# Dealing the first loads of a fused attention and GLU kernel to three DMA queues, and storing its last tile in three pieces

## The chip, the core and the metric

The kernel runs on one core of one Trainium2 chip. The metric is the device time of one execution in microseconds; the profile's span is about 1.8 us shorter, since it starts with the first instruction. The median of the kernel before is 222.75 us. A run counts as slow here when it is more than 1.5% above the fastest run of the same kernel; ratios use the others, the fast runs alone, and the text says where a run is slow. The engines are called TensorE (PE in the profile; its weight loads are PEld), VectorE (DVE), ScalarE (ACT), GpSimd (POOL) and SyncE (SP).

## The reference

2048 tokens of 512 features are normalized, go through a linear attention with a softmax feature map (32 heads of 16 features) and, beside it, through a bilinear GLU of 1792 columns; the sum of both and the input is the output.

```python
xn = layernorm(x)                      # x: (1, 2048, 512), bf16
q, k, v = split(xn @ wqkv)             # wqkv: (512, 1536)
pq, pk = q @ w_phi, k @ w_phi          # per head, 16 x 16
phi_q = concat(softmax(pq), softmax(-pq)); phi_k = likewise
o = (phi_q @ (phi_k.T @ v)) / (phi_q @ sum(phi_k) + 1e-6)
out = x + o @ wo + ((xn @ w_gate) * (xn @ w_up)) @ w_down
```

## The kernel before

The kernel folds w_phi into the k part of wqkv ("W1k", from wk transposed and a block-diagonal BD made of wphi), so the first things that it needs are four token tiles (statistics on VectorE, transpose on TensorE), wv, then wk transposed and wphi, then the first 256 columns of the two GLU weights, wg and wu. A DMA is started by SyncE, ScalarE or GpSimd, each on its own queue. The opening:

```python
    dma_x(0, 1)                                   # token tile 0, SyncE
    dma_x(1, 2, nc.scalar)                        # token tile 1, ScalarE
    dma_x(2, 4)                                   # token tiles 2 and 3, SyncE
    dma_cols(wv, A_wqkv, 2 * D, 0, D, nc.scalar)
    dma_cols(wg, B_w_gate, 0, 0, 256, nc.sync)
    dma_cols(wu, B_w_up, 0, 0, 256, nc.sync)
    nc.sync.dma_start_transpose(out=wkT, in_=A_wqkv[:, D:2 * D])
    dma_x(4, 8)
    # ... further columns of wg and wu, tokens 8 to 15 ...
    # ... constants on GpSimd ...
    nc.gpsimd.dma_start(out=wphi[:], in_=A_w_phi.rearrange("(c h) d f -> (h d) c f", c=DC))
    # ...
    warmup(10)                                    # matmuls on zeros
    # ...
        LNs(0); LNr(0); LNs(1); LNr(1)            # statistics of tiles 0 and 1 (one call a line in the source)
        LNx(0); TRpe(0)                           # normalize and transpose tile 0
        LNs(2); LNr(2)                            # statistics of tile 2
        warmup(5, 1)
        LNx(1); TRpe(1)
        # ... Vm(0) with wv ..., then foldj(wkT, ...), then the first gate matmul G()
```

The last output tile was made in two pieces of 256 columns (`Fin(n, 2 if n == NT - 1 else 1)`), each with its own matmuls, addition and store.

Below, "the first fold" is the first matmul of `foldj`, which needs wk; the first gate matmul is the first that needs wg.

The softmax here doesn't subtract the row's maximum and nothing guards it: scores larger than these inputs give would overflow.

## Time and profile before

| | before |
|---|---|
| median of device times | 222.75 us |
| span of the profile | 221.0 us |
| TensorE busy | 214.8 us, 97% |
| TensorE's waits for another engine or a DMA | 2.1 us, all in the first 7 us |
| TensorE dense from | 6.73 us |
| wk transposed: issued, landed, first used | 2.78, 9.8, 10.89 us |

TensorE is the bound. A load matters only if TensorE, or what TensorE waits for, would have started sooner with it.

### The profile page before, as it was taken

The page shows a single profiled execution, that of the slowest core. Times are in us where ns is not written, and L with a number is a line of the kernel's source. Part 1 is how long each engine was busy: PE and PEld are TensorE (multiplying, and loading weights), DVE is VectorE, ACT ScalarE, POOL GpSimd, SP SyncE. Part 2 cuts the span into 40 slices and gives each one's busy share as a digit, 9 for nine tenths or more (in the row PEclk, how much of TensorE's full clock was granted, in tenths as well). Part 3 has the DMA queues.
Part 4 walks back from the last instruction along what each step waited for, and adds up shares of the span by engine and source line. Part 5 has one row for each costly group of instructions (what it writes and reads, how often), then busy time and mean ns, then how long its engine had stood idle before and what let it go on. Part 6 is the DMA issues. An engine that isn't in the chain of part 4 may idle for free.

```text
span 221.0 us, 3357 instructions
## 1 busy us (share of the span) xinstructions
PE 214.8 (97%) x1242; PEld 104.6 (47%) x1265; DVE 155.2 (70%) x273; ACT 86.7 (39%) x178; POOL 19.7 (9%) x31
## 2 busy tenths in 40 slices
PE   7999999999999999999999999999999999999994
PEld 2554445454445444544545444444444444444453
DVE  3679999999999999999898694847564128311121
ACT  3776457675666466738533443332020012000000
POOL 5000000000101110302110121111010000000000
PEclk9999999999999999999999999999999999999999
DMA  6999940694111714610472263731729602151001
GB/s 203 262 369 383 214 96 4 198 317 102 50 47 53 183 49 97 143 49 6 133 174 95 74 166 103 174 131 47 190 74 228 177 26 72 62 128 46 25 27 47
DMA packets 52272, 27.76 MB, mean 126 GB/s; under 512 B 36496, under 2 KB 49184, under 8 KB 52256
## 3 DMA queue, kind: packets, MB, share of 16 engines
q1 hardware_dynamic: 51552, 26.88, 44.3%
q10 hardware_dynamic: 672, 0.66, 0.9%
q8 instruction: 10, 0.16, 0.3%
q14 instruction: 6, 0.05, 0.1%
q0 software_dynamic: 32, 0.02, 0.0%
HBM read 8.67 MB, written 9.96 MB: 84 GB/s over the span
## 4 chain that ended last, share of the span: by engine, by line
PE 95%; DVE 2%; DMA 1%; issue 1%; ACT 0%; ACTq 0%
PE gu L154 22%; PE gu L166 22%; PE gu L148 22%; PE pk L245 6%; PE gu L169 6%; PE pk L300 6%; PE vp L261 5%; PE kv L292 2%; PE kv L336 2%; DMA xall<-in_A_x_dram 1%; PE pk L261 1%; DVE stats L192 1%; PE pk L232 1%; PE gu L210 0%; DVE xn L203 0%
## 5 line engine op out<-in xcount | busy, mean ns | idle before, releaser
L151 ACT CAST g_sb<-gu 128x512 bf16<-128x512 f32 x56 | 32.8, 586 | 62.8 <-PE gu L148 57.4
L154 PE MATMUL gu<-xnT,wu 128*128 128x512 bf16 x220 | 56.9, 379 | 0.3
L148 PE MATMUL gu<-xnT,wg 128*128 128x512 bf16 x216 | 56.2, 379 | 0.5
L171 DVE TENSOR_TENSOR o_sb<-gu,xall 128x512 bf16<-128x512 f32 (+1 forms) x17 | 11.2, 660 | 41.3 <-PE gu L169 41.3
L154 PEld LDWEIGHTS <-wu 128*128 128x128 bf16 x224 | 21.9, 98 | 26.4
L148 PEld LDWEIGHTS <-wg 128*128 128x128 bf16 x224 | 20.9, 98 | 22.7 <-issue 0.2
L321 POOL TENSOR_TENSOR phiq<-eq,rho 128x512 bf16<-128x512 f32 x16 | 16.9, 1059 | 141.0 <-DVE rho L319 123.0
L287 DVE TENSOR_TENSOR phik<-e,rs 128x1024 bf16<-128x1024 f32 x16 | 20.1, 1255 | 0.7
L276 DVE TENSOR_REDUCE sums<-e 128x64 f32<-128x1024 f32 x16 | 19.3, 1206 | 0.0
L169 PE MATMUL gu<-wo,xnT 128*128 128x512 bf16 (+1 forms) x65 | 16.3, 366 | 0.1
L245 PE MATMUL pk<-W1k,xnT 128*128 128x512 bf16 x64 | 16.1, 379 | 0.0
L300 PE MATMUL pk<-W1q,xnT 128*128 128x512 bf16 x59 | 15.7, 379 | 0.2
L156 DVE TENSOR_TENSOR hT_97<-gu,g_sb 128x512 bf16<-128x512 f32 x14 | 9.6, 690 | 8.6 <-PE gu L154 7.8
L305 ACT ACTIVATE phiq<-pk 128x512 bf16<-128x512 f32 x16 | 9.6, 597 | 13.9 <-PE pk L300 9.0
L253 ACT ACTIVATE e<-pk 128x512 f32<-128x512 f32 x16 | 9.6, 598 | 12.0 <-PE pk L245 10.5
L261 PE MATMUL vp<-wv,xnT 128*128 128x512 bf16 x52 | 13.3, 379 | 0.0
L166 PE MATMUL gu<-wd,hT_97 128*128 128x512 bf16 (+1 forms) x69 | 12.9, 336 | 0.1
L166 PE MATMUL gu<-wd,hT_94 128*128 128x512 bf16 x56 | 12.7, 379 | 0.0
L166 PE MATMUL gu<-wd,hT_96 128*128 128x512 bf16 x55 | 12.7, 379 | 0.1
L166 PE MATMUL gu<-wd,hT_95 128*128 128x512 bf16 x55 | 12.7, 379 | 0.1
L192 DVE BATCH_NORM_STATS2 stats<-xall 128x6 f32<-128x512 bf16 x16 | 10.9, 680 | 2.5 <-DMA xall<-in_A_x_dram 2.5
L342 DVE TENSOR_TENSOR o_tok<-kv,rden 128x512 bf16<-128x512 f32 x16 | 11.1, 691 | 0.6
(75 smaller groups left out, 220.8 us busy)
## 6 DMA issues: line engine op xcount, KB each, us to landing
out_dram<-o_sb SPq DMA_DIRECT2D x15, 128.0 KB, 1.7
wd<-in_B_w_down_dram SPq DMA_DIRECT2D x1, 1792.0 KB, 8.2
xall<-in_A_x_dram SPq DMA_DIRECT2D x3, 512.0 KB, 11.9
wg<-in_B_w_gate_dram SPq DMA_DIRECT2D x1, 1024.0 KB, 8.6
wu<-in_B_w_up_dram SPq DMA_DIRECT2D x1, 1024.0 KB, 11.6
qd_780<-phiq SPq DMA_DIRECT2D x4, 256.0 KB, 2.7
qd_1207<-phiq SPq DMA_DIRECT2D x4, 256.0 KB, 2.0
qd_1510<-phiq SPq DMA_DIRECT2D x4, 256.0 KB, 2.0
```

Of the source, the lines that this page charges most:

```text
L148: nc.tensor.matmul(gps[:], lhsT=wg[:, c, f * P:(f + 1) * P], rhs=xnT[:, c, T * TT:(T + 1) * TT], start=(c == 0), stop=(c == DC - 1))
L151: nc.scalar.copy(out=g_sb[:], in_=gps[:])
L154: nc.tensor.matmul(ups[:], lhsT=wu[:, c, f * P:(f + 1) * P], rhs=xnT[:, c, T * TT:(T + 1) * TT], start=(c == 0), stop=(c == DC - 1))
L166: nc.tensor.matmul(fin[:], lhsT=hT[T][:, f, t4 * P:(t4 + 1) * P], rhs=wd[:, f, sl], start=(f == 0), stop=False)
L169: nc.tensor.matmul(fin[:], lhsT=oT[:, c, n * P:(n + 1) * P], rhs=wo[:, c, sl], start=False, stop=(c == DC - 1))
L192: nc.vector.bn_stats(out=stats[:], in_=xall[:, n, :])
L245: nc.tensor.matmul(pk[:], lhsT=xnT[:, j, n * P:(n + 1) * P], rhs=W1k[:, j, :], start=(j == 0), stop=(j == DC - 1))
L261: nc.tensor.matmul(vp[:], lhsT=xnT[:, j, n * P:(n + 1) * P], rhs=wv[:, j, :], start=(j == 0), stop=(j == DC - 1))
L276: nc.vector.tensor_reduce(out=sums[:], in_=ev, axis=AX.X, op=ALU.add)
L287: nc.vector.tensor_tensor(out=phik[:].rearrange("p k (h f) -> p (k h) f", f=DH), in0=ev, in1=rss[n][:].to_broadcast((P, 2 * H, DH)), op=AL ...
L300: nc.tensor.matmul(pq[:], lhsT=xnT[:, j, n * P:(n + 1) * P], rhs=W1q[:, j, :], start=(j == 0), stop=(j == DC - 1))
L321: nc.gpsimd.tensor_tensor(out=phiqs[n][:, :, 1, :].rearrange("p k (h f) -> p k h f", f=DH), in0=eqs[n][:].rearrange("p k (h f) -> p k h f" ...
```

## The change

The intent is that the loads which are wanted first no longer stand in one queue behind each other: tokens and the transposing load of wk alone on SyncE, the small wphi and then wv on ScalarE, the first GLU columns on GpSimd. At the other end, a smaller last piece lets the last addition and store be shorter.

```diff
     dma_x(0, 1)
-    dma_x(1, 2, nc.scalar)
+    nc.scalar.dma_start(out=wphi[:], in_=A_w_phi.rearrange("(c h) d f -> (h d) c f", c=DC))
+    dma_x(1, 2)
     dma_x(2, 4)
     dma_cols(wv, A_wqkv, 2 * D, 0, D, nc.scalar)
-    dma_cols(wg, B_w_gate, 0, 0, 256, nc.sync)
-    dma_cols(wu, B_w_up, 0, 0, 256, nc.sync)
     nc.sync.dma_start_transpose(out=wkT, in_=A_wqkv[:, D:2 * D])
     ...
-    nc.gpsimd.dma_start(out=wphi[:], in_=A_w_phi.rearrange("(c h) d f -> (h d) c f", c=DC))
+    dma_cols(wg, B_w_gate, 0, 0, 256, nc.gpsimd)
+    dma_cols(wu, B_w_up, 0, 0, 256, nc.gpsimd)
     ...
-    def Fin(n, parts=1):
+    def Fin(n, cuts=(0, D)):
     ...
-            Fin(n, 2 if n == NT - 1 else 1)
+            Fin(n, (0, 256, 384, D) if n == NT - 1 else (0, D))
```

More of the change, by code (lines that the diff above doesn't have):

```diff
@@ L156, in G @@
             nc.vector.tensor_tensor(out=hT[T][:, f, :], in0=ups[:], in1=g_sb[:], op=ALU.mult)
-    def Fin(n, parts=1):
+    def Fin(n, cuts=(0, D)):
         T, t4 = divmod(n, GT)
         o_sb = opool.tile([P, D], BF16, name="o_sb")
-        w = D // parts
-        for i in range(parts):
-            sl = slice(i * w, (i + 1) * w)
+        for lo, hi in zip(cuts, cuts[1:]):
+            w, sl = hi - lo, slice(lo, hi)
             fin = ps_gu.tile([P, w], F32, name="gu")
```

## The prediction

> **What bounds the kernel now.** I read the page's busy lines first, then TensorE's waits, then the chain that ended last at its two ends, then the DMA engines in slices of 0.2 to 0.4 us over the first 6 us.
>
> ```profile
> PE 214.8 (97%) x1242; PEld 104.6 (47%) x1265; DVE 155.2 (70%) x273; ACT 86.7 (39%) x178; POOL 19.7 (9%) x31
> PE   7999999999999999999999999999999999999994
> PE gu L132 <- DVE eps_t L107: 1.1, 1, 1.1
> PE gu L210 <- DVE xn L203: 1.0, 2, 0.5
> ```
>
> TensorE is busy for 214.8 of 221.0 us; only the first and the last of the 40 slices are not full. The last two lines are all that it waited for in the whole span. No wait is left in the middle, so the change can act only before TensorE becomes dense and after its last matmul; a load that comes sooner for a later use gains nothing.
>
> The chain at the start and at the end (start, duration, what):
>
> ```profile
> 0.81 2.71 DMA xall<-in_A_x_dram
> 3.55 0.71 DVE stats L192
> 4.46 0.59 DVE stats L192
> 5.25 0.30 DVE xn L203
> 5.55 0.61 DVE stats L192
> 6.19 0.18 DVE mv L194
> 6.37 0.31 DVE xn L203
> 6.73 0.40 PE gu L210 x4
> 7.12 0.86 PE pk L261 x4
> ...
> 217.59 0.45 PE gu L169 x4
> 218.04 0.02 issue
> 218.07 0.42 DVE o_sb L171
> ```
>
> From 6.73 us TensorE runs without a real gap. What puts 6.73 there is VectorE: statistics of token tile 0, of tile 1, normalizing tile 0, statistics of tile 2 (the 5.55 row; 5.47 in the timeline), normalizing tile 1, the transpose of tile 1. Each starts as soon as the last is done, so tiles 1 and 2 are in time now: tile 1 was issued at 0.81 and took 2.9 us (landing 3.71, wanted at 4.38), tiles 2 and 3 were issued at 1.20 and took 3.6 us (landing 4.80, wanted at 5.47, a slack of 0.67 us). The 5.47 is the number that matters: the statistics of tile 2 stand in VectorE's order ahead of the normalizing of tile 1, without which TensorE cannot go on.
>
> The issues (timeline) and what the DMA engines did, with SyncE's queue as q1 and ScalarE's as q10 (packets, MB, share of 16 engines), in the stretches 2.4 to 2.8, 4.8 to 5.0 and 5.2 to 5.4 us:
>
> ```profile
> 0.81 0.86 SPq L81 DMA_DIRECT2D xall<-in_A_x_dram  x2
> 1.24 0.47 ACTq L84 DMA_DIRECT2D wv<-in_A_wqkv_dram  x1
> 1.73 0.46 SPq L84 DMA_DIRECT2D wg<-in_B_w_gate_dram  x1
> ...
> q10 hardware_dynamic: 63, 0.06, 52.2%
> q1 hardware_dynamic: 65, 0.06, 45.8%
> ...
> q10 hardware_dynamic: 75, 0.08, 107.8%
> ...
> q1 hardware_dynamic: 66, 0.03, 55.7%
> q10 hardware_dynamic: 44, 0.04, 52.8%
> ```
>
> Tiles 0 and 1, issued together, share the engines packet by packet. But wg, issued on SyncE at 1.73 with nothing of its own queue before it after about 4.2, moves no packet while wv streams on ScalarE's queue, and starts at 5.2, when wv has some 50 of its 512 packets left. So a large load holds back a load issued after it on the other hardware queue: the two act nearly as one queue in order of issue.
>
> **What the Trainium skill says.** "DMA: Bandwidth & Descriptors", section "Issuing engines are not separate DMA queues", says that loads of all issuers run on the same 16 engines and interleave, and that more issuers save only issue time. The trace agrees for tiles 0 and 1 and differs for wg behind wv. "Perfetto Trace Analysis", section "DMA Instruction — HWDGE (DVE, Sync)", says that the block that makes the descriptors is shared between the sequencers that issue such loads; that fits wg's wait, though the issues themselves overlap in the timeline (1.20 and 1.24), so no lock shows there. "TensorE: Matmul & The Clock Gate", section "Part 1: The HAM clock gate (the "warmup" mystery)", says that the clock halves after an idle window of about 3.4 us. Gaps before 6.73 are 0.5 us here and the matmuls after them run at 0.86 us for four of 512 columns, so nothing of that shows.
>
> **The change part by part.**
>
> Start, order of the loads. SyncE now issues tile 0 (0.81), tile 1 (0.81 + 0.39 = 1.20, by the first issue's duration) and tiles 2 and 3 (about 1.60); ScalarE wphi (0.81) and wv (0.81 + about 0.47, the issue of wv itself, = 1.28). Before, tiles 2 and 3 were issued at 1.20, just ahead of wv at 1.24. Now they come 0.3 us behind wv, and by the reading above their packets follow wv's. In 1 KB packets the tokens 0 to 3 and wv are 128 + 128 + 256 + 512 = 1024. Before, the last of these, wv's, passed at about 5.45, with about 0.15 us of wg mixed in: the set ends near 5.3. To it comes wphi, which from ScalarE is 512 runs of 32 bytes. No row shows such packets from a hardware queue; the 256-byte packets of the transpose pass at 453 in 0.4 us, so I estimate 512 / 453 x 0.4 = 0.45 us. Tiles 2 and 3 then end near 5.75, and land 0.7 us later (wv took from 5.45 to 6.04, tiles 2 and 3 from about 3.98 to 4.80): 6.45. The statistics of tile 2 start at 6.45 instead of 5.47, **+1.0 us**, and the rest of the chain to TensorE's dense part follows unchanged.
>
> Start, tile 0. Without tile 1 beside it, it ends sooner: of its 128 packets some 42 had passed by 2.4 us (slices before that), the other 86 alone take, at the 350 per us of the next slices, 0.25 us, plus as many small ones, 0.08, so 2.73 instead of 2.92, and VectorE starts about 0.15 us sooner. This counts only if tiles 2 and 3 are not what comes last. Tile 1 lands near 4.2, against a need of 4.2 to 4.4: no matter.
>
> Weights. wphi (landed 8.1, wanted 9.71) and transposed wk (landed 2.78 + 7.0 = 9.8, wanted 10.89) come sooner: no gain, since nothing waits for them. The first GLU columns go to GpSimd at 2.29 and 3.2. wphi took 5.8 us from there; with 2 us more for 256 KB each in a shared stream I estimate landings near 10 and 11, wanted at 12.0 and 12.65. No cost, but less slack.
>
> End. The last tile is 256, 128, 128 columns instead of 256, 256. Matmuls of 256 columns follow each other in 1.53 / 14 = 0.109 us, of 128 columns in 0.22 / 4 = 0.056 (the fold's rows): 36 x 0.056 - 18 x 0.109 = +0.05 us. The last addition shrinks from 0.42; 512 columns take 0.69, so 128 columns take 0.42 - 0.27 / 2 = 0.285, -0.135. The last store is half as large; 64 KB moved in about 0.2 us, I allow -0.05. Sum **-0.13 us**.
>
> Together 222.75 + 1.0 - 0.13 = 223.6.
>
> **The rivals.** (a) The queues are served side by side. Then tiles 2 and 3 share with wv, land near 5.1 and are in time; the gain of tile 0 stays, 222.75 - 0.15 - 0.13 = 222.5. For it: tiles 0 and 1 interleaved evenly. Against it: wg's wait of over a microsecond. (b) wphi's 512 small packets cost more than estimated, and GpSimd's wg joins while tiles 2 and 3 pass: each microsecond goes straight to the end, 224.2 to 224.6. For it: a first use of such packets. Against: in before GpSimd's data only began at 6.0. (c) First GLU columns late: TensorE stops at the first gate matmul near 12 us; 223 to 226. Against: 2 us of slack, and more if TensorE starts late. (d) The gap before TensorE's dense part grows to about 1.3 us and the clock halves for a while, +1.7 us. Against: it is well under 3.4 us.
>
> **Range and chances.** I give about 0.75 to tokens held behind wv (223.0 to 224.4) and 0.25 to rival (a). Shaded a little toward (a), the point is 223.5 and the range 222.5 to 224.3. A change of 2% is 4.5 us; only (c) and (d) together come near, and a gain of that size has nothing to come from: 0.003 faster, 0.987 same, 0.01 slower.
>
> **What would show it.** Right: in the chain of the changed kernel a DMA of tokens ends last a second time, ahead of the third statistics, at 6.0 to 6.9; TensorE waits about 1.5 us more for normalized tokens; q1 nearly empty while q10 carries wv; from the first gate matmul on, the middle as long as before. Wrong: third statistics at 5.3 to 5.5 with no wait before them, or any wait of TensorE for wg or wu. For the end: last addition near 0.28 us, and last matmul to end of span shorter by about 0.15 to 0.2.

## The result, and the profile after

The changed kernel takes 230.8 us in the median of six runs, 228.42 to 233.0; the kernel before took 222.76 in the same rounds. The ratio of the fast runs is 1.030, with a 95% interval of 1.024 to 1.036. Ratios here and below are the mean time of one kernel's fast runs over that of the other's of the same rounds, so not quite the ratio of the medians. The profiled run took 228.5 us with a span of 226.8, so it is one of the shorter ones; two of the six, 232.08 and 233.0, count as slow. Their mean granted clock, 0.985, is that of two fast runs too, so they may be the same effect at its longest; with them the ratio would be 1.034. Outside the range, and by far: 8 us lost instead of 0.75.

The slices of the page (busy tenths and granted clock in 40 slices):

```profile
PE   8659999999999999999999999999999999999995
PEclk9889999999999999999999999999999999999999
```

and what TensorE waited for (us in total, times, longest):

```profile
PE kv L231 <- DMA qT<-in_A_wqkv_dram: 2.4, 1, 2.4
PE gu L209 <- DVE xn L202: 2.1, 1, 2.1
```

The third wait of this list, 1.1 us before the warm-up, is as before.

The loss lies in the second and third slice, 5.7 to 17 us. From there on it is the old picture. There are two waits in it, and a clock below full in both slices. The chain tells which of these sets the end (start, duration, what):

```profile
2.19 14.58 DMA qT<-in_A_wqkv_dram
16.77 0.05 issue
16.82 0.40 PE kv L231 x4
...
223.79 0.24 PE gu L168 x4
...
224.05 0.29 DVE o_sb L170
```

There is no token, no VectorE and no matmul of wv in the chain any more. After SyncE's first issues it is one DMA: the transposing load of wk, issued at 2.19 and landed at 16.77, after 14.58 us instead of 7.0. The first fold stands at 16.82 instead of 10.89, and that difference, 5.93 us, less what the end gains, is the difference of the spans (226.8 - 221.0 = 5.8).

That is 5.8 of the 8 us by which the median grew. The rest is in runs of which no trace was kept. Four of the other five runs have a mean clock of 0.985 against 0.992 in the traced one, about twice the loss of clock; the trace of glu_gpsimd_first below shows a half clock after the wait for wk, which the traced run here does not have.

Where did 14.58 us come from? The DMA engines in the stretch from 8 to 10 us (queue, packets, MB, share of 16 engines; q1 is SyncE's queue, q0 GpSimd's), first before, where a small part is already the next load. The last line of it is wk's own load, 7.0 us from issue to landing. The shares add up the times of single packets, so they can pass 100%.

```profile
DMA packets 1514, 0.48 MB, mean 240 GB/s; under 512 B 1382, under 2 KB 1514, under 8 KB 1514
q1 hardware_dynamic: 1514, 0.48, 110.2%
...
qT<-in_A_wqkv_dram SPq DMA_TRANSPOSE x1, 7.0
```

and after:

```profile
DMA packets 455, 0.26 MB, mean 131 GB/s; under 512 B 417, under 2 KB 417, under 8 KB 455
q0 software_dynamic: 41, 0.16, 98.4%
q1 hardware_dynamic: 414, 0.11, 37.7%
```

The packets under 512 B are those of the transposing load, 256 B each, 2048 in all. In the same two microseconds 1382 of them passed before and 414 now, although the engines are as busy as before (98.4% and 37.7% against 110.2%). GpSimd's 41 packets, 4 KB each or a little less, hold 98.4% of 16 engines for 2 us: 0.984 x 32 / 41 = 0.77 us for one packet. The two GLU loads themselves land late (KB, us from issue to landing):

```profile
wg<-in_B_w_gate_dram POOLq DMA_DIRECT2D x1, 256.0 KB, 12.1
wu<-in_B_w_up_dram POOLq DMA_DIRECT2D x1, 256.0 KB, 13.4
```

The other wait is the one that the prediction was about: the statistics of tile 2 start at 7.17 us instead of 5.47, since tokens 2 and 3 land 5.4 us after their issue. This wait lies wholly inside the wait for wk and cost nothing in this run.

So the theory to test is: **GpSimd's loads and the transposing load of wk, in flight together, hold each other up; the loss is how late wk comes.** Its rivals: the late tokens begin the loss, through the gap and the clock; the 512 tiny packets of wphi do it; any two loads from two queues do it, or any small packets.

### The profile page after: what moved, and what is told of

It reads as the page before. It is cut to its first block, busy times and chain, and to the rows that moved or that the text cites.

```text
span 226.8 us, 3396 instructions
## 1 busy us (share of the span) xinstructions
PE 217.2 (96%) x1260; PEld 106.1 (47%) x1283; DVE 155.5 (69%) x274; ACT 87.0 (38%) x178; POOL 20.5 (9%) x32
## 4 chain that ended last, share of the span: by engine, by line
PE 91%; DMA 6%; issue 1%; SPq 1%; ACT 0%; DVE 0%; ACTq 0%
PE gu L154 21%; PE gu L165 21%; PE gu L148 21%; DMA qT<-in_A_wqkv_dram 6%; PE pk L244 6%; PE gu L168 6%; PE pk L299 6%; PE vp L260 5%; PE kv L291 2%; PE kv L335 2%; SPq L81 1%; PE pk L231 0%; ACT phiq L304 0%; PE kv L231 0%; DVE o_sb L170 0%
## 5 line engine op out<-in xcount | busy, mean ns | idle before, releaser
L170 DVE TENSOR_TENSOR o_sb<-gu,xall 128x512 bf16<-128x512 f32 (+2 forms) x18 | 11.4, 632 | 41.0 <-PE gu L168 41.0
L168 PE MATMUL gu<-wo,xnT 128*128 128x512 bf16 (+2 forms) x69 | 16.5, 354 | 0.1
L165 PE MATMUL gu<-wd,hT_97 128*128 128x512 bf16 (+2 forms) x83 | 13.1, 307 | 0.1
## 6 DMA issues: line engine op xcount, KB each, us to landing
wu<-in_B_w_up_dram SPq DMA_DIRECT2D x1, 1024.0 KB, 14.6
```

Source lines behind the costliest of these rows:

```text
L165: nc.tensor.matmul(fin[:], lhsT=hT[T][:, f, t4 * P:(t4 + 1) * P], rhs=wd[:, f, sl], start=(f == 0), stop=False)
L168: nc.tensor.matmul(fin[:], lhsT=oT[:, c, n * P:(n + 1) * P], rhs=wo[:, c, sl], start=False, stop=(c == DC - 1))
L170: nc.vector.tensor_tensor(out=o_sb[:, sl], in0=fin[:], in1=xall[:, n, sl], op=ALU.add)
```

## The experiments

Eleven kernels ran, in four calls; each call had its own runs of the kernel before (medians 222.87 to 222.98, scattering more than in the first measurement). All outputs passed the comparison with the reference. So did those of the two kernels that load wk untransposed: the comparison's tolerance doesn't see the difference that wk makes.

**tail_alone.** Only the last tile in three pieces.

```diff
-            Fin(n, 2 if n == NT - 1 else 1)
+            Fin(n, (0, 256, 384, D) if n == NT - 1 else (0, D))
```

> Only the last output tile in three pieces. From the traces of before and after: last addition 0.29 instead of 0.42 us, 0.05 us more of matmuls, the last store a little shorter. Every theory of the slowdown puts it into the start, so this must be 0.1 to 0.2 us faster than before (222.6). If it is slower by more than 0.1 us, the end took part in the loss.

Measured: 222.63 us (21 runs, 222.51 to 222.75) against 222.92 in the same rounds, ratio 0.9983 (0.9976 to 0.9990). The runs of before scatter upward to 223.61 there; against the first measurement, 222.75, it is 0.12. The end of the kernel is a small gain and has no part in the loss.

**glu_on_gpsimd.** Only the GLU columns moved, behind wphi.

```diff
-    dma_cols(wg, B_w_gate, 0, 0, 256, nc.sync)
-    dma_cols(wu, B_w_up, 0, 0, 256, nc.sync)
     ...
     nc.gpsimd.dma_start(out=wphi[:], ...)
+    dma_cols(wg, B_w_gate, 0, 0, 256, nc.gpsimd)
+    dma_cols(wu, B_w_up, 0, 0, 256, nc.gpsimd)
```

> Only the first GLU columns moved from SyncE to GpSimd, behind wphi, which stays there; tokens and wv as before. Theory M (GpSimd's loads and the transposing load of wk hold each other up): wk lands at 14 us or later instead of 9.8, TensorE waits for it before the first fold, the time is 4 to 8 us longer, 227 to 231. Rival T (the tokens behind wv start the loss, by the gap and the halved clock): tokens are in time here, so 222.7 to 223.2. Rival P (the 512 runs of 32 bytes of wphi on a hardware queue clog the engines): wphi is not on a hardware queue here, so 222.7 to 223.2 too.

Measured: 223.81 us (223.35 to 224.12), ratio 1.0038. A miss: well short of what the theory had said, though over both rivals' range. wk landed at 11.57 us, 1.8 later than before, and TensorE waited 0.6 us for it. The trace suggests why it was so little: with wphi ahead of them, the GLU packets began to flow at about 8 us, and by then some 1590 of the 2048 packets of the transpose had passed. Not all of the 1.8 us is due to these packets: from 5.75 to 6.25 us only 87 packets of the transpose passed, before GpSimd's first one. That called for an experiment that starts the overlap sooner (glu_gpsimd_first).

**tokens_behind_wv.** Only the new order of tokens, wphi and wv.

```diff
     dma_x(0, 1)
-    dma_x(1, 2, nc.scalar)
+    nc.scalar.dma_start(out=wphi[:], ...)
+    dma_x(1, 2)
     dma_x(2, 4)
     ...
-    nc.gpsimd.dma_start(out=wphi[:], ...)
```

> Only the new order of tokens, wphi and wv; GLU columns back on SyncE, the end as before. My prediction's own step: tokens 2 and 3 land at 6.2 to 7.2 us instead of 4.8, TensorE becomes dense 1.0 to 1.8 us later, plus up to 1.8 us if the clock halves for a while as it did in the changed kernel. Theory M: no more than that, 223.7 to 226, and wk lands before 11.5. Rivals T and P: the whole loss, 228 to 231.

Measured: 225.3 us in three runs and 223.47 in one, ratio 1.0087. wk landed at 10.7 and nothing waited for it, so neither the late tokens nor wphi's packets bring the loss of the changed kernel. The chain of the profiled run:

```profile
1.72 5.02 DMA xall<-in_A_x_dram
6.74 0.02 issue
6.76 0.71 DVE stats L192
...
8.64 1.71 PE pk L261 x4
```

and its stretches of two microseconds (length, then busy time and number of instructions of PE, PEld, DVE, ACT and POOL, then granted clock, DMA share and GB/s):

```profile
6.00:8.00 2.00, 0.00 (x0) 0.00 (x0) 1.20 (x4) 0.61 (x2) 0.00 (x0) 0.89 1.70 288
8.00:10.00 2.00, 1.97 (x8) 1.01 (x9) 1.34 (x4) 1.19 (x5) 0.00 (x0) 0.50 0.79 181
```

Tokens 2 and 3 land at 6.74, behind wv, as predicted (6.45). But the four matmuls of 512 columns that follow take 1.71 us where they took 0.86: TensorE had nothing to do for 2.1 us, and its clock was at half from about 7.5 to 11 us. The one run of 223.47 kept a mean clock of 1.0; the others had 0.991 or 0.992.

**tokens_kept_warm.** The same with the gap filled.

```diff
-        warmup(5, 1)
+        warmup(9)
```

> tokens_behind_wv with nine full warm-up matmuls in place of five small ones before the transpose of tile 1, to fill the gap in which TensorE waits for tokens 2 and 3. If about 1.1 us of its 2.4 us loss came from the halved clock in the 8 to 11 us stretch, the clock stays full and the time is 224.0 to 224.4. If the clock was no part of it, 225.3 as in tokens_behind_wv.

Measured: 223.97 us (eight runs, 223.64 to 224.51, clock 1.0 in all), ratio 1.0038. The four matmuls take 0.86 us again. So the late tokens alone cost 223.97 - 222.98 = 1.0 us, and the halved clock 1.3 us more.

**plain_wk.** The changed kernel with the old end, and wk loaded by a plain copy; the result is wrong.

```diff
-    nc.sync.dma_start_transpose(out=wkT, in_=A_wqkv[:, D:2 * D])
+    nc.sync.dma_start(out=wkT, in_=A_wqkv[:, D:2 * D].rearrange("(c p) n -> p c n", p=P))
```

> The changed kernel with the end of before, and wk loaded by an ordinary copy of the same 512 KB in place of the transposing load: wrong result on purpose. Theory M in the form that it takes a transpose on the other queue: GpSimd's two loads land by 9 or 10 us instead of 14.4 and 16.6, wk too, and what is left is the late tokens: 223.7 to 226. Rival M2 (GpSimd's loads are slow beside any hardware load): GpSimd's loads still land after 13 us and TensorE waits for them at the first gate matmul, 226 to 231.

Measured: 226.0 us (224.03 to 226.88, the shortest with full clock), ratio 1.0126: what tokens_behind_wv loses, and 0.7 more. The DMA engines from 8 to 10 us:

```profile
DMA packets 476, 0.65 MB, mean 326 GB/s; under 512 B 28, under 2 KB 413, under 8 KB 476
q1 hardware_dynamic: 388, 0.39, 63.6%
q0 software_dynamic: 88, 0.26, 40.0%
```

Beside plain loads a packet of GpSimd takes 0.400 x 32 / 88 = 0.145 us instead of 0.77, the engines move 326 GB/s instead of 131, and the GLU columns land at 9.2 and 10.2 us. GpSimd's queue is not slow in itself. TensorE's only waits are for the late tokens.

**glu_gpsimd_first.** Tokens in time, but GpSimd's first GLU load is issued at 2.3 us as in the changed kernel, wphi going to ScalarE behind wv.

```diff
     dma_cols(wv, A_wqkv, 2 * D, 0, D, nc.scalar)
+    nc.scalar.dma_start(out=wphi[:], ...)
-    dma_cols(wg, B_w_gate, 0, 0, 256, nc.sync)
-    dma_cols(wu, B_w_up, 0, 0, 256, nc.sync)
     ...
-    nc.gpsimd.dma_start(out=wphi[:], ...)
+    dma_cols(wg, B_w_gate, 0, 0, 256, nc.gpsimd)
+    dma_cols(wu, B_w_up, 0, 0, 256, nc.gpsimd)
```

> As glu_on_gpsimd, tokens in time, but wphi goes to ScalarE behind wv, so that GpSimd's first GLU load is issued about 1 us sooner, at 2.3 us as in the changed kernel. In glu_on_gpsimd the GLU packets began to flow at about 8 us, when some 1590 of the 2048 packets of the transposing load of wk had passed; here they should begin near 7 with some 1000 left. Theory M (the loss goes with the overlap of the two): wk lands after 12.5 us, the time is 225 to 230, clearly over the 223.8 of glu_on_gpsimd. Rival L (the overlap costs about 1 us whatever its size, and the rest of the loss of the changed kernel comes with the late tokens): 223.3 to 224.3.

Measured: 231.66 us (229.63 to 232.74), ratio 1.0371. TensorE's longest wait and the head of the chain:

```profile
PE kv L232 <- DMA qT<-in_A_wqkv_dram: 4.9, 1, 4.9
...
1.73 14.17 DMA qT<-in_A_wqkv_dram
```

The whole loss is there with tokens in time. One microsecond sooner on GpSimd, against glu_on_gpsimd, made a difference of 8 us. The edit also moves wphi's packets, which here pass on ScalarE from about 5.3 to 6.8 us, beside the transpose; but in the changed kernel they had landed by 3.2 us and the loss is there too, and plain_wk_256 below has them in the same place without it. Not all of the loss is the wait: after the 4.9 us the clock is 0.50 from 16 to 18 us, and from the first fold to the first matmul with the folded weight (L245) it takes 19.97 - 15.95 = 4.0 us, against 19.45 - 16.82 = 2.6 in the changed kernel at full clock. So 1.4 us of this run's loss is clock.

This kernel is not faster than the changed one (230.8), and no token is in the chain of either. So nothing shows that the late tokens of the changed kernel add to its loss: of two delays of the same engine that run at the same time the longer one counts.

**glu_on_scalar.** The same columns on ScalarE's hardware queue behind wv.

```diff
-    dma_cols(wg, B_w_gate, 0, 0, 256, nc.sync)
-    dma_cols(wu, B_w_up, 0, 0, 256, nc.sync)
+    dma_cols(wg, B_w_gate, 0, 0, 256, nc.scalar)
+    dma_cols(wu, B_w_up, 0, 0, 256, nc.scalar)
```

> The first GLU columns on ScalarE's hardware queue behind wv, issued near 1.8 and 2.3 us, the rest as before, so that they share the engines with the transposing load from another queue. Theory M in the form that it takes GpSimd's queue: wk lands near 10 us or a little later by what passes first, 222.5 to 223.5. Rival Q (any second queue beside the transposing load): wk lands after 12 us, 225 to 230.

Measured: 224.82 us in the median of six (223.67 to 225.2 in the five fast runs, 227.11 in a slow one), ratio 1.0062. wk landed at 12.46 us and TensorE waited 1.4 us for it. Between the two expectations: a second hardware queue beside the transposing load delays it too, though here wg passed ahead of the transpose and only wu met it. From 8 to 9 us, 165 of wu's 512-byte packets held 62.2% of the engines, 0.060 us each, against 0.031 for wg's and the last of wv's from 5 to 6, when the transpose was not yet flowing (528 packets, 103.8%). So the effect is not GpSimd's alone. Whether GpSimd's packets make it larger is not shown: only 256 KB met the transpose here, 512 KB in glu_gpsimd_first, and half_on_gpsimd, with 256 KB from GpSimd, has wk at 12.38 us in its trace, though its other runs are longer.

**half_on_gpsimd.** glu_gpsimd_first with wg back on SyncE, only wu on GpSimd.

```diff
+    dma_cols(wg, B_w_gate, 0, 0, 256, nc.sync)
     nc.sync.dma_start_transpose(out=wkT, ...)
     ...
-    dma_cols(wg, B_w_gate, 0, 0, 256, nc.gpsimd)
```

> As glu_gpsimd_first, but only the first up columns go to GpSimd, 256 KB instead of 512; the first gate columns stay on SyncE, ahead of the transposing load of wk. If the loss goes with how many GpSimd packets meet the transposing load, wk lands between before (9.8 us) and glu_gpsimd_first (15.9), near 12 to 14, and the time lies between, 224.5 to 228. If any GpSimd load in that stretch spoils the transpose as a whole, 229 to 232 as there. If 256 KB still fit beside it, 222.8 to 223.5.

Measured: 224.45, 226.44, 228.19 and 230.39 us; the last two count as slow, which leaves a ratio of 1.0114 from two runs (1.020 with all four; the slow ones, with clocks of 0.992 and 0.985, may again be the effect itself). In the profiled run, the 224.45, wk landed at 12.38. The loss lies between none and all, but the scatter of 6 us is as large as the effect, so it supports a dose no further than that.

**plain_wk_256.** glu_gpsimd_first with wk by plain copies in runs of 256 bytes, as many packets of the same size as the transposing load has; wrong result.

```diff
-    nc.sync.dma_start_transpose(out=wkT, in_=A_wqkv[:, D:2 * D])
+    for a in range(DC):
+        nc.sync.dma_start(out=wkT[:, :, a * P:(a + 1) * P],
+                          in_=A_wqkv[:, D + a * P:D + (a + 1) * P].rearrange("(c p) n -> p c n", p=P))
```

> glu_gpsimd_first (tokens in time, 231.7) with wk loaded by four ordinary copies in runs of 256 bytes, 2048 packets of the size that the transposing load has; wrong result on purpose. If it is the transposing itself that does not go beside GpSimd's packets, GpSimd's two loads land by 11 us, wk by 11.5, and the time is 222.7 to 224.5. If small packets of any kind do it, wk and GpSimd's loads land after 13 us and the time is 226 to 232.

Measured: 223.18 us (twelve runs, 222.72 to 223.71) against 222.87, ratio 1.0007 (0.9991 to 1.0022), so the same as before. Beside the 1.1 us before the warm-up TensorE has one wait:

```profile
PE gu L212 <- DVE xn L205: 0.4, 1, 0.4
```

There is none for wk or the GLU columns, which landed at 8.6 and 9.4 us. Same queues, same bytes, same packet size as glu_gpsimd_first, and GpSimd's loads are issued at the same times: the transposing is gone, and with it 8.5 us. (wk's four issues together take 2.26 us on SyncE instead of 4.98, so the later loads of SyncE start sooner: tokens 4 to 7 at 4.03 instead of 6.76. There is more traffic beside GpSimd's loads here, not less.) So the cause is the transposing load and the GLU loads in flight together; neither does it alone.

**one_queue** and **one_queue_8** were meant to beat both kernels: tokens, wv, GLU columns and wk in this order on SyncE, wphi on GpSimd, the new end; the second with eight warm-up matmuls.

```diff
-    dma_x(1, 2, nc.scalar)
+    dma_x(1, 2)
     dma_x(2, 4)
-    dma_cols(wv, A_wqkv, 2 * D, 0, D, nc.scalar)
+    dma_cols(wv, A_wqkv, 2 * D, 0, D, nc.sync)
     ...
-    warmup(10)
+    warmup(8)          # one_queue_8 only
```

> A version meant to beat both: tokens 0, 1, 2 and 3, then wv, GLU columns and wk, all on SyncE in this order, wphi on GpSimd as before, the last tile in three pieces. Tile 0 alone at the start landed at 3.05 us in the changed kernel, 0.48 sooner than in before; with tokens 2 and 3 ahead of wv nothing later should hold the chain, so TensorE becomes dense near 6.3 us instead of 6.73, and 0.15 comes at the end: 222.1 to 222.5. If the issues on one queue come too late (wv issued at 2.1 instead of 1.24), wv is what TensorE waits for: 222.6 to 223.5.

> one_queue with eight instead of ten warm-up matmuls. In one_queue TensorE was still in its warm-up until 5.51 us, half a microsecond after tile 0 was normalized, and became dense at 6.76. With eight (0.43 us each) the first transpose runs near 5.0, the second near 6.25: 222.1 to 222.4, the best version. If the warm-up is then too short for the full clock, the first matmuls run at half speed: 223 to 225 in some or all runs.

Measured: one_queue 222.83 us (222.25 to 223.39) against 222.98, ratio 0.9984; one_queue_8 223.05 us (222.78 to 224.27) against 222.92, ratio 1.0017. Tile 0 does come sooner (its statistics start at 2.97 us in one_queue instead of 3.55), but in one_queue TensorE is still in its warm-up until 5.51, and the first fold is only 0.24 us sooner (10.65 us instead of 10.89; 10.67 in one_queue_8). That lead is lost again by 33 us: there the chains of both have a transposing load of later tokens (in one_queue from 27.95 to 33.06 us), where that of tail_alone has TensorE alone; in one_queue_8 a matmul waited 0.4 us for it. Neither beats tail_alone: by ratio one_queue (0.9984) and tail_alone (0.9983) are level. What tail_alone wins is 0.12 us against the first measurement of before and 0.29 against that of its own rounds.

## Why the prediction was wrong

**The step that failed is "Weights."** It said that wk, issued sooner, comes sooner and that the GLU columns from GpSimd have "No cost, but less slack", with landings near 10 and 11 us. They landed at 14.4 and 16.6, and wk at 16.77 instead of 9.8. I had looked at when each load was issued and when it was wanted, and not at what the transposing load would share the engines with. In the kernel before it met no other stream of that size: wg and wu stood ahead of it on the same queue and had passed. The change took them out of that order and put them beside it. plain_wk_256 against glu_gpsimd_first shows that it takes the transposing (223.18 against 231.66), glu_on_gpsimd against glu_gpsimd_first that it takes an early overlap (223.81 against 231.66). Rival (c), late GLU columns, named the right loads but the wrong victim: TensorE never waited for them.

**The tokens held behind wv: right in size, and in mechanism only in part.** Predicted +1.0 us; tokens_kept_warm measures 1.0. In tokens_behind_wv the tokens did wait behind wv: from 3.25 to 4.75 us ScalarE's queue moved 334 packets and SyncE's 17. But the sum has luck in it. Its 0.45 us for wphi did not delay the tokens ahead of wv: from 2 to 3 us 221 packets of SyncE passed beside wphi's, where 226 in all passed before. Instead the engines moved 154 GB/s from 3.25 to 4.0 us, against 335 before, which the prediction did not have and which costs, as an estimate from these two rates, 0.4 us (0.75 x 181 / 335). In the changed kernel the two queues shared evenly from 4.8 to 5.4 us (113 and 109 packets), so the sign "q1 nearly empty while q10 carries wv" failed there. Its third statistics start at 7.17, a little beyond the 6.0 to 6.9 given, and it does not show in the time, because wk is later still.

**The clock: dismissed wrongly.** Rival (d) was set aside because the gap is "well under 3.4 us". The gap was 2.1 us. The clock was halved in the trace of tokens_behind_wv, three of its four runs have a mean clock of 0.991 or 0.992, and it cost 1.3 us. In the changed kernel it is hidden as well: the matmuls of wv at half clock were done before wk came.

**Tile 0 sooner:** its statistics start 0.48 us sooner in the changed kernel, not 0.15, again without use. **wphi's packets:** as time of the engines the estimate of 0.45 us holds roughly (as a delay it does not, see above); in the stretch from 2 to 3 us ScalarE's queue, nearly all of it wphi, has 539 packets in 39.6% of the engines. **The end:** the last addition took 0.29 us (predicted 0.285), from the last matmul to the end of the span 2.78 us instead of 2.96, the matmuls 0.05 longer: -0.13, as summed.

**What stays open:** why packets from another queue and those of a transposing load slow each other so much. The traces show packet times (0.77 against 0.145 us) and no cause inside the DMA engines. Nor is it shown what about the other loads matters: the queue, the packet size or the number of bytes. The transposing load can also stall by itself: from 8.0 to 8.75 us, with no other queue moving, 42 packets passed in tokens_behind_wv and 848 in tokens_kept_warm, which has the same loads in the same order. The scatter of the affected kernels, 228.4 to 233.0 us for the changed one, is not explained either; such stalls, the clock and a collision whose start varies all fit it, but no run tests that.

## What to carry to other kernels

When a load is moved to another queue, ask not only when it arrives but which loads it will now be in flight with, and above all whether one of them is a transposing load; one with a microsecond of slack can become the bound. Queues also give an order: what stood ahead of a transposing load in its queue could not meet it. And a gap of two microseconds in TensorE's work can cost more than the gap, because of the clock; warm-up matmuls in the gap took that part away here.

## What the Trainium skill lacked or had wrong

- "DMA: Bandwidth & Descriptors", section "Rules for kernel authors", says "A transpose next to ordinary DMAs needs nothing". It stands in the row on two transposes that corrupt each other (the comparison here, which does not see wk, can say nothing on that); no page that I read gives the cost in time of such a neighbour: beside 512 KB of GpSimd loads the transposing load landed after 14.6 us instead of 7.0, GpSimd's packets took 0.77 us instead of 0.145, and the kernel lost 8 us. With plain copies of the same packet size the loss is gone (ratio 1.0007).
- The same page, section "Issuing engines are not separate DMA queues": loads of all issuers interleave. In the changed kernel they did from 4.8 to 5.4 us (113 and 109 packets of two queues). But the page lacks that a load can also be held behind an earlier one of another queue: in tokens_behind_wv, with tokens 2 and 3 issued 0.4 us behind wv, 334 packets of wv's queue passed from 3.25 to 4.75 us and 17 of theirs, and they landed at 6.7 us instead of 4.8.
- "TensorE: Matmul & The Clock Gate", section "Part 1: The HAM clock gate (the "warmup" mystery)", has the clock halve after an idle window of about 3.4 us. Here less was enough: a wait of 2.1 us in tokens_behind_wv (225.3 us in three of four runs, 223.47 with full clock in the fourth) and one of 1.5 us in plain_wk, where the clock fell at 9.0 us, 0.8 us after TensorE had begun again. Each of the four half-clock stretches traced (also in the changed kernel and glu_gpsimd_first) lasted about 3.4 us.
